# Cosformer attention into a mixture of experts on one core: routing of the last chunks behind the fourth first layer, first gates for one rank alone, a weight load moved up, last products in banks of their own

## Chip, cores and metric

One Trainium2 chip, one of its cores. The metric is the device time of one execution in microseconds (us); lower is better. The kernel before took 336.34 us (median of 3 runs, 334.81 to 336.97).

## The reference, cut to what matters

```python
# q, k, v: (8, 8, 576, 64); moe weights: w_gate, w_output_gate (512, 8), w1 (8, 512, 1024), w2 (8, 1024, 512)
attn = linear attention with cos/sin position weights      # -> x: (4608 tokens, 512)
logits = x @ w_gate
e_idx  = argmax(logits, axis=1)                            # one expert for a token
gate_w = softmax(logits)[token, e_idx]
eom    = sigmoid(x @ w_output_gate)
for e in range(8):
    m = e_idx == e
    out[m] = gate_w[m] * eom[m, e] * (relu(x[m] @ w1[e]) @ w2[e])
```

The draw is fixed. It gives the experts 305, 493, 580, 0, 986, 569, 398 and 1277 tokens.

## The kernel before

Attention runs in 36 units of 128 tokens, and its rows are written ("scattered") into regions of DRAM, one for each expert. Then the rows come back in 39 tiles of up to 128 tokens of one expert: gather (`xg`), transpose (`x_tr`), first layer, transpose (`h_tr`), second layer, output. A chunk is the 128 rows of one scatter, an eviction is VectorE's copy of a second layer's product out of PSUM (`ysb`), and a gate is a wait for a rank's weights (`wait_ge` on `wsem`). Experts are ranked; ranks 0 to 3 have their weights loaded before or about the end of attention, ranks 4 to 7 during the tiles. Tiles 0 to 7 are fixed early ("early table"); the gathers of tiles 8 and later need the late table and all scatters.

All scatters, weight loads and outputs are issued by GpSimd, on one DMA queue. The gathers are issued by SyncE. A weight load reads 2 MB of float32 and writes 1 MB of float16.

```python
def x_tr(j):                        # transpose the rows of tile j, wait for its weights
    ...
    if j < 2:
        lim = (32, 48)              # 32: rank 0 is loaded; 48: rank 1 too
    ...
    for m, n in enumerate(lim):
        DVE.wait_ge(wsem[m], n)
    DVE.tensor_copy(xts, xp16)

def layer2(j):
    ...
    yp = yps[0][:, j % 2, :]        # two banks of one PSUM tile
    ...                             # 8 matmuls, eviction on DVE (ysb)
    GP.indirect_dma_start(out=out, in_=ysb, ...)

# after attention; j counts tiles, "late" builds the late table, step() is routing of the last 5 chunks
layer1(0); x_tr(2); layer1(1); h_tr(0); ...; layer1(2); h_tr(1); x_tr(3)
step()                              # first stage, VectorE only
layer2(0); scatter(3, 2); scatter(3, 3)
step(3)                             # the stage with matmuls (rk) and what follows
layer2(1); step()
scatter(3, 4); scatter(3, 5)
for j in range(3, NMAIN + 1):
    h_tr(j - 1); x_tr(j + 1)
    for _ in range(2 if j < 6 else 0):
        next(late, None)
    layer1(j)
    for c in {3: (6, 7), 4: (8,)}.get(j, ()):
        scatter(3, c)
    layer2(j - 1)                   # (j - 2 for tiles that are transposed by DMA)
    fetch(...)                      # gathers: tiles 8 and 9 at j = 5
    for w in wload.get(j, ()):      # {4: [(4, 1)], 5: [(4, 0)], 6: [(5, 0)], ...}: (rank, half)
        load_w(*w)
```

Of the kernel before, what the change touches and what calls it, by code (L numbers as in the profile page):

```python
# [10 lines left out]
F32 = mybir.dt.float32  # L11
# [10 lines left out]
def kernel(  # L22
# [23 lines left out]
    P = 128  # L46
    NC4 = 4
    NG = B // 2
# [5 lines left out]
    NMAIN = 39  # L54
# [151 lines left out]
    def load_w(r, m):  # L206

        if r not in wreg:
            wreg[r] = GP.value_load(ordi[0:1, r:r + 1], min_val=0, max_val=E - 1)
            if r > 1:  # L210

                GP.wait_ge(wsem[r % 2], 16 * (r % 2) + 32 * (r // 2))
        er = wreg[r]
        if m == 0:
            d = GP.dma_start(w1v[:, r], moe_w1[bass.ds(er, 1)].rearrange(
                "o (c p) f -> p (o c) f", p=128))
        else:
            d = GP.dma_start(w2v[:, r], moe_w2[bass.ds(er, 1)].rearrange(
                "o (c p) d2 -> p (o c) d2", p=128))
        d.then_inc(wsem[r % 2], 16)  # L220
        tc.declare_no_dep(d.ins, group="mm", reason="ranks loaded before")
        tc.add_to_no_dep_group("w", d.ins)
# [25 lines left out]
    ptr = ctx.enter_context(tc.tile_pool(name="ptr", bufs=2, space=bass.MemoryType.PSUM))  # L248
    if True:
# [295 lines left out]
        def scatter(g, c):  # L545

            di, meta, xrows, c0, c1 = scat[g]
            if c == c0:
                GP.tensor_copy(xrows[:, c0:c1, DM:DM + 4].bitcast(F32), meta[:])
            else:  # L550
                GP.nop()
            d = GP.indirect_dma_start(
                out=xs[:, :],
                out_offset=bass.IndirectOffsetOnAxis(ap=di[:, c - c0:c - c0 + 1], axis=0),
                in_=xrows[:, c, :], in_offset=None)


            tc.declare_no_dep(d.ins, group="sc", reason="distinct rows")
            tc.declare_no_dep(d.ins, group="early", reason="distinct rows")
            tc.add_to_no_dep_group("sc", d.ins)  # L560
# [73 lines left out]
        def late_valid():  # L634

            sp = ptr.tile([P, 512], F32, name="shift", tag="tr")
            PE.matmul(sp[:, 0:NL], onesf[:], dgs[:], start=True, stop=True)
            DVE.tensor_scalar(valid[:], sp[:, 0:NL], pv[:, 0:1], None, ALU.is_le)
# [23 lines left out]
        def late_table():  # L662
            counts("l")
            yield
            ti = small("ti@l", [P, E], I32)
            DVE.tensor_scalar(ti[:], prm[:, 2, 0:E], 127.0, None, ALU.add)
            DVE.tensor_single_scalar(ti[:], ti[:], 7, op=ALU.arith_shift_right)
            tl = small("tl@l", [P, E])
            DVE.tensor_tensor(tl[:], ti[:], tk[:], ALU.subtract)
            pin = prefix("l", tl[:])  # L670
            DVE.tensor_copy(nlate[:], pin[:, E - 1:E])
            yield
            DVE.tensor_tensor(tl[:], tl[:], pin[:], ALU.subtract)
            DVE.tensor_tensor(prm[:, 0, 0:E], tl[:], tk[:], ALU.add)
            yield from table("l", tabs[1], pin)
# [3 lines left out]
        yps = []  # L679
# [13 lines left out]
        def x_tr(j):  # L693
            xg = xgs[j]
            xps = ptr.tile([P, 512], F32, name=f"xtsp{j}", tag="tr")
            xp16 = xps[:, 0:256].bitcast(F16)
            for kc in range(4):
                PE.transpose(xp16[:, kc * 128:(kc + 1) * 128],  # L698
                             xg[:, kc * 128:(kc + 1) * 128].bitcast(F16), ident16[:, :])

            if j < 2:

                lim = (32, 48)
            elif j < 22:
                tab, jj = (tabs[0], j) if j < EARLY else (tabs[1], j - EARLY)
                lim = nc.values_load_multi_w_load_instructions(
                    tab[jj:jj + 1, 0:2], engines=(mybir.EngineType.DVE,),
                    min_val=16, max_val=144)[1]
            else:
                lim = (128, 144) if j == 22 else ()  # L710
            for m, n in enumerate(lim):
                DVE.wait_ge(wsem[m], n)
            xts = fsb.tile([P, 4, P], F16, name=f"xts{j}", tag="xts")
            DVE.tensor_copy(xts[:].rearrange("p k t -> p (k t)"), xp16)  # L714
            xtss[j] = xts
            if j >= EARLY:
                jj = j - EARLY
                DVE.copy_predicated(sidx[:, jj:jj + 1], valid[:, jj:jj + 1],
                                    xg[:, DM:DM + 2].bitcast(I32))
# [36 lines left out]
        def layer2(j):  # L756
            hts = htss.pop(j)
            ev = evr.pop(j)
            xg = xgs.pop(j)
            if not yps:  # L760
                yps.append(pkv.tile([P, 2, 512], F32, name="yps", tag="kvp"))
            yp = yps[0][:, j % 2, :]
            for fc in range(8):
                mm = PE.matmul(yp, hts[:, fc, :],  # L764
                               wt[:, bass.ds(ev, 1),
                                  4 * F + fc * DM:4 * F + fc * DM + DM],
                               start=(fc == 0), stop=(fc == 7))
                tc.declare_no_dep(mm.ins, group="w", reason="waits on wsem")
                tc.add_to_no_dep_group("mm", mm.ins)
            ysb = fsb.tile([P, DM], F32, name=f"ysb{j}", tag="ysb", bufs=5)  # L770
            DVE.tensor_scalar(ysb[:], yp, xg[:, DM + 2:DM + 4].bitcast(F32),  # L771
                              None, ALU.mult)
            idx = (xg[:, DM:DM + 2].bitcast(I32) if j < EARLY
                   else sidx[:, j - EARLY:j - EARLY + 1])
            d = GP.indirect_dma_start(  # L775
                out=out[:, :],
                out_offset=bass.IndirectOffsetOnAxis(ap=idx, axis=0),
                in_=ysb[:], in_offset=None,
                bounds_check=N - 1, oob_is_err=False)
            tc.declare_no_dep(d.ins, group="so", reason="distinct rows")  # L780
            tc.add_to_no_dep_group("so", d.ins)
# [11 lines left out]
        i = 0  # L793
# [70 lines left out]
        pending = []  # L864

        def step(n=1):
            for _ in range(n):
                for p in list(pending):
                    try:
                        next(p)  # L870
                    except StopIteration:
                        pending.remove(p)

        wload = {25: [(0, 0)], 26: [(0, 1)], 28: [(1, 0)], 29: [(1, 1)], 31: [(2, 0)],
                 32: [(2, 1)], 34: [(3, 0)]}
# [4 lines left out]
        for i, (b, c) in enumerate(units):  # L880
# [58 lines left out]
            if n == 8:  # L939
                pending.append(route(g, glog, xrows, *((0, GC) if g < 3 else (4, GC))))  # L940
            else:
                step({20: 1, 21: 2, 22: 3, 23: 0, 24: 3, 25: 0, 26: 0}.get(i, 1))

            if i == 30:
                first_half = route(g, glog, xrows, 0, 4)
# [42 lines left out]
            for w in wload.get(i, ()):  # L988
                load_w(*w)

        wload = {4: [(4, 1)], 5: [(4, 0)], 6: [(5, 0)], 7: [(5, 1)], 8: [(6, 0)],
                 9: [(6, 1)], 10: [(7, 0)], 12: [(7, 1)]}
        late = late_table()

# [13 lines left out]
        x_tr(3)  # L1008
        step()
        layer2(0)  # L1010
        scatter(NG - 1, 2)
        scatter(NG - 1, 3)
        step(3)
        layer2(1)
        step()
        assert not pending
        scatter(NG - 1, 4)
        scatter(NG - 1, 5)
        for j in range(3, NMAIN + 1):
            if j < NMAIN and j - 1 not in BY_DMA:  # L1020
                h_tr(j - 1)
            if j + 1 < NMAIN:
                x_tr(j + 1)

            for _ in range(2 if j < 6 else 0):
                next(late, None)
            if j < NMAIN:
                layer1(j)
            for c in {3: (6, 7), 4: (8,)}.get(j, ()):
                scatter(NG - 1, c)  # L1030

            for m in (j - 2, j - 1):
                if (m in BY_DMA) == (m == j - 2):
                    if j == NMAIN - 1 and m == j - 1:

                        h_tr(j)
                    layer2(m)
            if j == 6:
                late_valid()
            for jj in {5: [8, 9], 6: [10, 11]}.get(j, [j + 5]):  # L1040
                if 5 <= j and jj < NSLOT:
                    fetch(jj)
            if j in BY_DMA:
                h_tr(j)
            for w in wload.get(j, ()):
                load_w(*w)
        with tc.If(nc.values_load(nlate[0:1, 0:1], min_val=0, max_val=NL) >  # L1047
                   NMAIN - EARLY):
            x_tr(NMAIN)
# [40 lines left out]
```

## Time and profile before

| | |
|---|---|
| median of 3 runs | 336.34 us |
| TensorE, VectorE, ScalarE, GpSimd busy | 90, 58, 44, 40% |
| attention's last product starts | 157.03 us |
| from there to tile 7's first layer | 42.3 us |
| from there to the end of the span | 137.9 us |

The last two rows are "the head" (from attention's last product to tile 7's first layer, 199.37 - 157.03) and "the rest" (337.3 - 199.37). The lines of the profile are in the prediction.

### The profile page before, as it was taken

To read this page: it belongs to the slowest core of one execution; us is meant where nothing else is said; L and a number is where in the kernel's file an instruction comes from. 1 tells how busy PE (TensorE), PEld (TensorE's weight loads), DVE (VectorE), ACT (ScalarE), POOL (GpSimd) and SP (SyncE) were. 2 spreads that over 40 slices of the span, in tenths; PEclk is the share of its full clock that TensorE was granted. 3 is DMA by queue.
4 is the path that set the end of the run, shared out by engine and by line. 5 is a ranking of instruction groups with operands and counts; after the bars stand their busy time and mean duration, and the time that the engine had idled before them with its cause. 6 is when DMAs were issued, how large, how long until landed. Compare 5 with 4: busy or idle time off the path is not lost. (4 is left out here: it accounts for less than half of the span.)

```text
span 337.3 us, 8923 instructions
## 1 busy us (share of the span) xinstructions
PE 303.6 (90%) x3032; PEld 198.4 (59%) x3032; DVE 194.8 (58%) x547; ACT 148.3 (44%) x253; POOL 136.5 (40%) x171
## 2 busy tenths in 40 slices
PE   7998899999999889987948789998989999999980
PEld 2577788888787778865514445554544444444530
DVE  6667568975788997965867534444343323422330
ACT  3246798877787678535301222221223232223210
POOL 7002224318833576576776443433121322232231
PEclk9999999999999999999979999999999999999997
DMA  8999999987996588999999299999997979776711
GB/s 184 312 295 313 275 230 313 235 249 205 318 247 184 167 219 156 219 221 230 228 229 232 100 196 240 225 246 254 246 245 173 200 171 191 171 172 159 174 46 47
DMA packets 83164, 71.81 MB, mean 213 GB/s; under 512 B 36078, under 2 KB 75566, under 8 KB 83120
## 3 DMA queue, kind: packets, MB, share of 16 engines
q1 hardware_dynamic: 65568, 40.17, 48.2%
q0 software_dynamic: 17552, 31.05, 41.0%
q8 instruction: 28, 0.46, 0.6%
q14 instruction: 16, 0.13, 0.1%
HBM read 67.61 MB, written 16.17 MB: 248 GB/s over the span
## 5 line engine op out<-in xcount | busy, mean ns | idle before, releaser
L754 ACT ACTIVATE hs<-hp 128x1024 f16<-128x1024 f32 x39 | 39.9, 1023 | 116.9 <-PE hp L746 107.7
L764 PE MATMUL yps<-wt,hts 128*128 x312 | 75.0, 384 | 3.7 <-DVE ysb L771 1.5
L771 DVE TENSOR_SCALAR ysb<-yps,xg 128x512 f32<-128x512 f32 x39 | 29.3, 751 | 83.1 <-PE yps L764 78.0
L746 PE MATMUL hp<-wt,xts 128*128 x312 | 73.7, 379 | 3.3 <-DVE xts L714 2.0
L468 POOL TENSOR_TENSOR xr<-wt,rc 128x512 f16<-128x512 f32 x36 | 40.5, 1132 | 66.7 <-DVE rc L464 59.4
L775 POOL DMA_INDIRECT out_dram<-ysb,sidx x31 | 30.2, 975 | 79.4 <-DVE ysb L771 76.8
L764 PEld LDWEIGHTS <-hts 128*128 128x128 f16 x312 | 30.8, 99 | 41.6 <-issue 4.8
L445 PE MATMUL qo<-kvm,wt 64*128 64x162 f32 (+1 forms) x640 | 50.5, 310 | 3.2 <-DVE wt L453 2.2
L746 PEld LDWEIGHTS <-xts 128*128 128x128 f16 x312 | 29.1, 98 | 31.6 <-DVE xts L714 2.2
L445 PEld LDWEIGHTS qo<-kvm,wt 64*128 64x128 f32 (+1 forms) x640 | 40.7, 175 | 10.2 <-DVE wt L453 3.7
L451 ACT ACTIVATE wt<-qo,cosc 128x324 f32<-128x324 f32 x72 | 36.9, 528 | 19.7 <-PE qo L445 17.1
L453 DVE SCALAR_TENSOR_TENSOR wt<-qo,sinc,wt 128x324 f32<-128x324 f32 x72 | 37.0, 550 | 12.9 <-ACT wt L451 8.5
L427 PE MATMUL qtp<-ident,wt 128*64 128x128 f32 x576 | 40.0, 279 | 0.5 <-ACT wt L406 0.5
L427 PEld LDWEIGHTS qtp<-ident,wt 128*64 128x64 f32 x576 | 30.9, 136 | 7.5 <-issue 6.5
L382 PE MATMUL kvp<-wt 128*64 128x130 f32 x448 | 31.2, 277 | 0.9 <-ACT ktr L335 0.8
L382 PEld LDWEIGHTS kvp<-wt 128*64 128x64 f32 x448 | 25.3, 136 | 2.3 <-issue 1.1
L714 DVE COPY xts<-xtsp 128x512 f16<-128x512 f16 x39 | 16.3, 420 | 13.4 <-DMA wt<-in_moe_w_dram 5.2
L431 DVE TENSOR_SCALAR wt<-qtp 128x512 f32<-128x512 f32 x32 | 21.8, 681 | 1.4 <-PE qtp L427 1.4
L336 ACT ACTIVATE wt<-wt,cosc 128x512 f32<-128x512 f32 x28 | 20.0, 713 | 0.6 <-DMA wt<-in_v_dram 0.6
L335 ACT ACTIVATE wt<-wt 128x512 f32<-128x512 f32 x28 | 17.5, 624 | 1.9 <-PE kvp L382 1.9
L340 ACT ACTIVATE wt<-wt,sinc 128x512 f32<-128x512 f32 x24 | 17.2, 715 | 0.0
L698 PE MATMUL xtsp<-ident,xg 128*128 128x128 f16 x156 | 14.9, 219 | 1.4 <-DMA xg<-xs 1.4
(271 smaller groups left out, 302.1 us busy)
## 6 DMA issues: line engine op xcount, KB each, us to landing
wt<-in_moe_w_dram POOLq DMA_DIRECT2D x16, 1024.0 KB
wt<-in_k_dram SPq DMA_DIRECT2D x16, 512.0 KB
wt<-in_v_dram SPq DMA_DIRECT2D x16, 512.0 KB
wt<-in_q_dram SPq DMA_DIRECT2D x16, 512.0 KB
xg<-xs SPq DMA_DIRECT2D x43, 129.0 KB
xs<-zt SPq DMA_DIRECT2D x9, 129.0 KB
wt<-in_k_dram SPq DMA_DIRECT2D x8, 128.0 KB
vtb<-in_v_dram SPq DMA_DIRECT2D x8, 128.0 KB
```

The lines of the kernel that those rows point to most:

```text
L382: PE.matmul(kvp[64 * ab:64 * ab + 64, s_ // 2, o:o + 130], kr[p0:p1, head(s_, ab), :], vw[p0:p1, head(s_, ab), :], start=(c == 0 and s_ % ...
L427: PE.matmul(tp[64 * ab:64 * ab + 64, 128 * s_:128 * s_ + 128], src[:, head(s_, ab), :], ident[:], start=True, stop=True)
L431: DVE.tensor_scalar_max(qT2[i % 2], tps, 0.0)
L445: PE.matmul(qo[t0:t1, 2 * ab + s_, 0:162], qT[r0:r0 + 64, s2, t0:t1], kvms[b if c < 4 else b - 1 + j][r0:r0 + 64, 2 * s2:2 * s2 + 2, :], s ...
L451: d0 = ACT.activation(t, qo[:, :, 0:81], AF.Copy, scale=cosc[:, c:c + 1])
L453: d1 = DVE.scalar_tensor_tensor(u[:, h0:h0 + 4, :], qo[:, :, 81:162], sinc[:, c:c + 1], t, ALU.mult, ALU.add)
L468: GP.tensor_tensor(xrows[:, slot + x, 0:DM].bitcast(F16).rearrange("p (h d) -> p h d", d=D), u[:, 8 * x:8 * x + 8, 0:64], rc[:, 8 * x:8 * ...
L746: mm = PE.matmul(hp[:, fh * 512:fh * 512 + 512], xts[:, kc, :], wt[:, bass.ds(ev, 1), kc * F + fh * 512:kc * F + fh * 512 + 512], start=(k ...
L754: ACT.activation(hs[:], hp, AF.Relu)
L764: mm = PE.matmul(yp, hts[:, fc, :], wt[:, bass.ds(ev, 1), 4 * F + fc * DM:4 * F + fc * DM + DM], start=(fc == 0), stop=(fc == 7))
L771: DVE.tensor_scalar(ysb[:], yp, xg[:, DM + 2:DM + 4].bitcast(F32), None, ALU.mult)
L775: d = GP.indirect_dma_start(out=out[:, :], out_offset=bass.IndirectOffsetOnAxis(ap=idx, axis=0), in_=ysb[:], in_offset=None, bounds_check= ...
```

## The change

The intent: take the routing's matmuls out of TensorE's way (they stood ahead of tile 1's second layer), start tiles 0 and 1 when rank 0's weights are there, fill a hole in the DMA with an earlier weight load, and free the last two second layers of a wait for the eviction before them. The early routing steps are also dealt out anew.

```diff
@@ x_tr
-                lim = (32, 48)
+                lim = (32,)
@@ layer2
-            yp = yps[0][:, j % 2, :]
+            if NMAIN - 2 <= j < NMAIN:
+                yp = ptr.tile([P, 512], F32, name=f"yp{j}", tag="tr")[:]
+            else:
+                yp = yps[0][:, j % 2, :]
@@ attention units
-                step({20: 1, 21: 2, 22: 3, 23: 0, 24: 3, 25: 0, 26: 0}.get(i, 1))
+                step({20: 2, 21: 0, 22: 2, 23: 0, 24: 3, 25: 1, 26: 0}.get(i, 1))
@@ loads
-        wload = {4: [(4, 1)], 5: [(4, 0)], 6: [(5, 0)], ...
+        wload = {3: [(4, 1)], 5: [(4, 0)], 6: [(5, 0)], ...
@@ tiles
         scatter(NG - 1, 3)
-        step(3)
         layer2(1)
-        step()
-        scatter(NG - 1, 4)
-        scatter(NG - 1, 5)
         for j in range(3, NMAIN + 1):
             ...
-            for _ in range(2 if j < 6 else 0):
-                next(late, None)
             if j < NMAIN:
                 layer1(j)
-            for c in {3: (6, 7), 4: (8,)}.get(j, ()):
+            if j == 3:
+                step(4)
+            for _ in range({3: 1, 4: 2, 5: 3}.get(j, 0)):
+                next(late, None)
+            for c in {3: (4,), 4: (5, 6), 5: (7, 8)}.get(j, ()):
                 scatter(NG - 1, c)
+            for w in wload.get(j, ()):
+                load_w(*w)
             ...                      # layer2, fetch
-            for w in wload.get(j, ()):
-                load_w(*w)
```

In GpSimd's order this puts the load (4,1), half of rank 4, ahead of the scatters of chunks 5 to 8. The kernel before issues it behind all of them.

More of the change, by code (lines that the diff above doesn't have):

```diff
@@ L989 @@
                 load_w(*w)
-        wload = {4: [(4, 1)], 5: [(4, 0)], 6: [(5, 0)], 7: [(5, 1)], 8: [(6, 0)],
+        wload = {3: [(4, 1)], 5: [(4, 0)], 6: [(5, 0)], 7: [(5, 1)], 8: [(6, 0)],
                  9: [(6, 1)], 10: [(7, 0)], 12: [(7, 1)]}
@@ L1012 @@
         scatter(NG - 1, 3)
-        step(3)
         layer2(1)
-        step()
-        assert not pending
-        scatter(NG - 1, 4)
-        scatter(NG - 1, 5)
         for j in range(3, NMAIN + 1):
@@ L1023 @@
                 x_tr(j + 1)
-            for _ in range(2 if j < 6 else 0):
-                next(late, None)
             if j < NMAIN:
                 layer1(j)
-            for c in {3: (6, 7), 4: (8,)}.get(j, ()):
+            if j == 3:
+                step(4)
+                assert not pending
+            for _ in range({3: 1, 4: 2, 5: 3}.get(j, 0)):
+                next(late, None)
+            for c in {3: (4,), 4: (5, 6), 5: (7, 8)}.get(j, ()):
                 scatter(NG - 1, c)
+            for w in wload.get(j, ()):
+                load_w(*w)
             for m in (j - 2, j - 1):
```

## The prediction

> **What bounds the kernel now.** I read the page first, then TensorE's idle time in order of time, then VectorE and GpSimd where TensorE waits, then busy time in stretches of 1 us for the DMA share.
>
> ```profile
> PE   7998899999999889987948789998989999999980
> DMA  8999999987996588999999299999997979776711
> ```
>
> Each digit is 8.4 us. TensorE is at 8 or 9 nearly everywhere; its weak slices are number 20 and 21 (160 to 177 us) and a few after them. The DMA engines are full from about 120 to 250 us, but for one slice, the "2" at 185 to 194 us. Attention ends at 158 us; then 39 tiles of 128 tokens follow, each a first layer (line 746) and a second (line 764). The tiles run at a beat of 4.12 us up to number 17 (193.65 for tile 6 against 189.53 for tile 5) and 3.68 us later (304.86 to 308.53). From 231 us to the last tiles TensorE has one idle of 0.90 us and no other, so what is gained before it can reach the end, if no wait swallows it on the way.
>
> The timeline of TensorE (start, duration, then in brackets the idle time before it):
>
> ```profile
> 157.03 1.34 PE L445 MATMUL qo<-kvm,wt 64*64 64x162 f32 x32 [0.24 <-DVE wt L453]
> 160.35 1.89 PE L746 MATMUL hp<-wt,xts 128*128 x8 [1.99 <-DVE xts L714]
> ...
> 173.24 0.20 PE L511 MATMUL rk<-oh,u 128*128 128x48 f16 x1 [4.49 <-DVE oh L503]
> 173.81 3.15 PE L764 MATMUL yps<-wt,hts 128*128 x8 [0.25 <-DVE ysb L771]
> 177.47 1.89 PE L746 MATMUL hp<-wt,xts 128*128 x8
> ...
> 198.57 0.40 PE L698 MATMUL xtsp<-ident,xg 128*128 128x128 f16 x4 [0.71 <-DMA xg<-xs]
> 199.37 1.89 PE L746 MATMUL hp<-wt,xts 128*128 x8 [0.40 <-issue]
> ...
> 229.41 0.40 PE L698 MATMUL xtsp<-ident,xg 128*128 128x128 f16 x4 [0.67 <-DMA xg<-xs]
> 230.21 1.89 PE L746 MATMUL hp<-wt,xts 128*128 x8 [0.40 <-issue]
> ```
>
> The reader is to see three kinds of loss: waits on VectorE at 158 and 169 us (1.99, 4.49 and 0.25), a second layer at 3.15 instead of 1.89 us, and two waits for gathered rows (xg, tiles 8 and 15). The same view at the end of the span shows the last two second layers waiting for evictions:
>
> ```profile
> 324.48 1.89 PE L764 MATMUL yps<-wt,hts 128*128 x8 [0.40 <-DVE ysb L771]
> 327.21 1.89 PE L764 MATMUL yps<-wt,hts 128*128 x8 [0.84 <-DVE ysb L771]
> ```
>
> VectorE's timeline for the first two waits:
>
> ```profile
> 159.77 0.76 DVE L714 COPY xts<-xtsp 128x512 f16<-128x512 f16 x2 [2.32 <-DMA wt<-in_moe_w_dram]
> 170.67 1.73 DVE L497 TENSOR_TENSOR oh@3_4_2622<-glog,lmax@3_4_2618 128x40 f32<-128x40 f32 x1
> 172.90 0.20 DVE L503 TENSOR_TENSOR oh<-iota8m,ei@3_4_2625 128x40 f16<-128x40 f32 x1
> 173.02 0.74 DVE L771 TENSOR_SCALAR ysb<-yps,xg 128x512 f32<-128x512 f32 x1
> ```
>
> The copy at 159.77 waited for the weights of rank 1, though tiles 0 and 1 use rank 0. That rank 0 is there sooner: the load of rank 2 is issued at 151.28 behind a wait for rank 0. And the eviction at 173.02 stands behind the routing's first stage in VectorE's order.
>
> GpSimd's timeline, where all scatters (552), weight loads (215, 218) and outputs (775) are issued:
>
> ```profile
> 142.98 1.04 POOL L552 DMA_INDIRECT xs<-xr,di@2_0_2158  x1 [0.28 <-POOL xr L549]
> 160.42 1.00 POOL L552 DMA_INDIRECT xs<-xr,di@2_0_2158  x1 [2.76 <-DMA xs<-xr,di@2_0_2158]
> 186.73 0.98 POOL L552 DMA_INDIRECT xs<-xr,di@3_4_2679  x1 [0.30 <-issue]
> 192.02 0.94 POOL L218 DMA_DIRECT2D wt<-in_moe_w_dram  x1 [0.94 <-PE hp L746]
> ```
>
> The issue at 160.42 waits for the DMA eight before it, by the instruction order the scatter of 142.98. That scatter, 128 rows, took 17 us: it was done just after rank 1's weights, issued right ahead of it, had landed at 159.7. So a scatter behind a weight load waits for the load. And in busy time by 1 us, the hole in the DMA:
>
> ```profile
> 189.00:190.00 1.00, 1.00 (x13) 0.68 (x11) 0.93 (x2) 0.00 (x0) 0.00 (x0) 1.00 0.00 0
> ```
>
> The last two columns are the DMA share and GB/s: nothing moves between the last scatter (186.73) and the next weight load (192.02).
>
> **What the Trainium skill says.** "TensorE: Matmul & The Clock Gate", Part 1: after an idle window of about 3.4 us the array runs at half clock until it has been busy for such a window. The trace agrees: granted clock 0.50 from 173 to 176 us, after the 4.49 us of idle. "SBUF — State Buffer", section "SBUF: two separate sides": VectorE and GpSimd share a port pair as an exclusive lock; the other fully blocks. The trace agrees: line 497 took 1.73 us instead of the 0.20 of its neighbours, and ended at 172.40 with GpSimd's line 468 (171.28 to 172.33). "DMA: Bandwidth & Descriptors", section "Queues, rings and completion order": on each DMA engine, descriptors are consumed in ring order. The scatter of 142.98 agrees; this one carries my prediction.
>
> **The change, part by part.**
>
> *First gates for rank 0 alone.* The copies at 159.77 can follow the last line 453 before them (ends 157.46): xts0 is ready at about 157.9, before attention's last product ends at 158.37. The first layer starts there: -1.99 us.
>
> *Routing behind the fourth first layer.* Only its later stages move. The first stage (lines 491 to 503) keeps its place ahead of the eviction of tile 0 on VectorE, and the second layer of tile 1 waits for that eviction, since both outputs are halves of one buffer (the 0.25 of before). So most of the 4.49 stays: everything shifts by 1.99, and if GpSimd's line 468 no longer meets line 497, 1.5 more is gone. TensorE then idles from 166.8 to about 170.5, 3.7 us, so the half clock may or may not come. I take the second layer of tile 1 at 170.5 to 171.5 and the first layer of tile 3 at about 173.3: -4.2 us. From there to tile 7's first layer before took 21.9 us, of which 16.5 are four beats, the rest late evictions and tile 8's rows. With late routing spread over tiles 3 to 5, I count about 18 us (VectorE still delays one second layer by some 0.7): tile 8's rows would be wanted at about 191 and tile 7 could start near 192, -7.4 us in all.
>
> *Weight loads.* Half of rank 4 (4,1) is issued after tile 3's first layer, about 179 instead of 192 us, into the hole. But it now stands ahead of four scatters (chunks 5 to 8), and tile 8's gather waits for the last of these. The second half of rank 3 lands at about 181 (GB/s jumps to 330 and 400 at 181 to 183, which are plain copies). Then in ring order: three scatters and two outputs, 0.9 MB, at about 350 GB/s 2.6 us; the 1 MB load, about 5 us (four loads took 24 us with other traffic from 160); 1.05 MB of outputs and scatters, 3 us. That is 191.6, and a microsecond for completion: the gather is issued at about 192.5, where it was issued at 192.95 before. It landed 5.6 us later then. So tile 8's rows come at about 198, and of the 7.4 us some 6.5 turn into a longer wait there. Tile 7 starts at 198.7 or so: -0.7 us.
>
> *After it.* Tile 15's rows wait for the output of tile 7 (its buffer), which before was behind (4,1), (4,0), (5,0), (5,1), counted from 194 when the DMA restarts, to 223.6: 29.6 us. After the change it is behind (4,0), (5,0), (5,1), (6,0), since loads are now issued ahead of outputs: as much data, but from 192. So 221.6, rows at 227; tile 14 reaches them at 227.3 and starts at about 228, against 230.21: -2.2 us. Beyond that TensorE is the bound as before.
>
> *Last products in banks of their own.* The waits of 0.40 and 0.84 go: -1.24 us, straight off the end.
>
> *Early routing steps* (units 20 to 26) move four VectorE operations away from a stall of 1.17 us at 112 us to a place just ahead of a copy on the chain. I give it 0, within 0.7, and what comes of it is swallowed at tile 8.
>
> Sum: 2.2 + 1.24 = 3.4 us; 336.34 - 3.4 = 332.9, rounded to 333.0.
>
> **Rivals.** *The queue does not hold the scatters up* (they overlap with the load). Then tile 8's rows come at about 191 to 193 and the 7.4 us reach the end, with 1.24 more: 327.7 us. For it: the table of late tiles is ready at about 187 instead of 191.84. Against: the scatter of 142.98. *The queue costs more*: (4,1) and the gathers share full DMA engines and each output is one load further back; if tile 8's rows come at 200.5 and tile 15's at 230.5, nothing but the tail is left or less: 335 to 336.5. For it: DMA share 1.1 from 195 to 248 us. *The old VectorE stage keeps everything*: the idle crosses the clock window again, so tile 3 gains 2 instead of 4 us; as the rows of tile 8 set the pace, that makes 333 all the same.
>
> **Range and chances.** The two DMA steps decide. Both at their worst give 336, the rival without queueing 327.7; I take 329.0 to 336.0. Faster by over 2% needs 329.6 or less: that takes at least half of the swallowed time to come through, 0.15. Slower by 2% needs 343, which nothing here makes: 0.02. Within: 0.83.
>
> **What would show it.** Right: first layer of tile 0 at 158.4 us; the idle before tile 1's second layer still 3 to 4.5 us and released by the eviction; no DMA hole at 185 to 194; a wait of 4 to 7 us for xg before tile 8's transposes, or a gather issued at about 192; no idle between the last three second layers. Wrong: tile 8's rows at 193 or sooner (then about 328), or a first layer of tile 14 later than 230 (then 335 or more).

## The result, and the profile after

The changed kernel took 344.49 us (median of 4 runs, 344.13 to 345.46); the kernel before 335.67 us in the same session. Ratios here are the mean time of one kernel's fast runs over that of the other's of the same rounds, so not quite the ratio of these medians: 1.0264, with a 95% interval of 1.0219 to 1.0309. The change makes the kernel slower by 2.6%.

The profiled spans are 337.3 us before and 342.6 us after, 5.3 us apart and not 8.8: the profiled run of before (338.99 us) was slower than all its timed ones. The head grew from 42.3 to 52.5 us; the rest shrank from 137.9 to 134.5 us.

TensorE's timeline after the change, the lines that answer to those shown before:

```profile
157.33 1.89 PE L746 MATMUL hp<-wt,xts 128*128 x8 [0.45 <-issue]
...
171.47 3.57 PE L768 MATMUL yps<-wt,hts 128*128 x8 [5.69 <-DVE ysb L775]
...
176.12 1.92 PE L746 MATMUL hp<-wt,xts 128*128 x8
...
206.90 0.61 PE L698 MATMUL xtsp<-ident,xg 128*128 128x128 f16 x4 [13.45 <-DMA xg<-xs]
208.02 2.99 PE L746 MATMUL hp<-wt,xts 128*128 x8 [0.51 <-issue]
...
330.52 3.62 PE L768 MATMUL yp<-wt,hts 128*128 x16
```

Tile 0 starts at once (0.45 instead of 1.99 us). Tile 1's second layer waits even longer than before, and for the eviction. Tile 8's rows then keep TensorE idle for 13.45 us, and the first layer after that runs partly at half clock (2.99 us). From there to the end there is no idle at all: the waits of before at tiles 13 to 15, at 245 us and at the last two second layers (now 16 matmuls in one piece) are gone. That is 4.5 us; less 1.1 us for the slow first layer, it is the 3.4 us of the rest.

VectorE after the change: the first stage of the routing, the eviction, and the end of the late table:

```profile
168.33 1.73 DVE L497 TENSOR_TENSOR oh@3_4_2620<-glog,lmax@3_4_2616 128x40 f32<-128x40 f32 x1
...
170.68 0.75 DVE L775 TENSOR_SCALAR ysb<-yps,xg 128x512 f32<-128x512 f32 x1
...
188.21 0.15 DVE L631 TENSOR_TENSOR tab<-cj@l,sel@l 128x1 int32<-128x1 f32 x1
```

The table is ready at 188.4, as against 191.84 before. GpSimd after the change: scatter of chunk 4, the load (4,1), and the last scatter:

```profile
181.98 0.98 POOL L552 DMA_INDIRECT xs<-xr,di@3_4_2736  x1 [0.86 <-POOL xr L549]
183.86 0.94 POOL L218 DMA_DIRECT2D wt<-in_moe_w_dram  x1 [0.90 <-DMA xs<-xr,di@3_0_2537]
...
191.54 0.97 POOL L552 DMA_INDIRECT xs<-xr,di@3_4_2736  x1 [0.30 <-issue]
```

And SyncE: the gather of tile 8 before the change, the gathers from that of tile 8 on after it, and from the list of SyncE's waits after it (us in total, times, longest) the one for the last scatters:

```profile
192.95 0.34 SPq L688 DMA_DIRECT2D xg<-xs  x1
```

```profile
200.40 5.40 SPq L688 DMA_DIRECT2D xg<-xs  x5
```

```profile
SPq L688 <- DMA xs<-xr,di@3_4_2736: 11.2, 1, 11.2
```

So the gather of tile 8 goes out at 200.40, 12 us after the table is ready, and for 11.2 of them it waits for the scatters, the last of which was issued at 191.54. In the kernel before, SyncE's list has no wait for these scatters; the gather follows the table (191.84) by 1.1 us. The trace's packet records say when they moved: the load (4,1) from 185.5 to 193.9 us, the scatters of chunks 5 to 8 with two outputs between them from 193.3 to 198.6. In the kernel before, the last scatter moved at 188.3 to 189.1, and the load from 193.7 to 202.6. The page's list of DMA issues gives the median time from issue to landing of the 16 weight loads in its last column, which the page of the kernel before does not have:

```profile
wt<-in_moe_w_dram POOLq DMA_DIRECT2D x16, 1024.0 KB, 12.6
```

### The profile page after: what moved, and what is told of

Read it like the earlier page. It is cut to its first block, busy times and chain, and to the rows that moved or that the text cites. A ratio compares the mean times of both kernels' runs of the same rounds, so it can differ in the third digit from the quotient of the medians.

```text
span 342.6 us, 8922 instructions
## 1 busy us (share of the span) xinstructions
PE 302.7 (88%) x3032; PEld 198.9 (58%) x3032; DVE 194.2 (57%) x547; ACT 148.5 (43%) x253; POOL 136.9 (40%) x171
## 5 line engine op out<-in xcount | busy, mean ns | idle before, releaser
L768 PE MATMUL yps<-wt,hts 128*128 x296 | 71.6, 386 | 6.1 <-DVE ysb L775 5.7
L746 PE MATMUL hp<-wt,xts 128*128 x312 | 74.8, 383 | 1.0 <-issue 1.0
L775 DVE TENSOR_SCALAR ysb<-yps,xg 128x512 f32<-128x512 f32 x37 | 27.8, 750 | 75.2 <-PE yps L768 75.2
L779 POOL DMA_INDIRECT out_dram<-ysb,sidx x31 | 30.2, 973 | 83.8 <-DVE ysb L775 83.0
L714 DVE COPY xts<-xtsp 128x512 f16<-128x512 f16 x39 | 16.3, 420 | 25.0 <-PE xtsp L698 14.2
L698 PEld LDWEIGHTS <-xg 128*128 128x128 f16 x156 | 11.4, 100 | 18.5 <-DMA xg<-xs 13.6
## 6 DMA issues: line engine op xcount, KB each, us to landing
wt<-in_moe_w_dram POOLq DMA_DIRECT2D x16, 1024.0 KB, 12.6
```

The lines of the kernel that those rows point to most:

```text
L698: PE.transpose(xp16[:, kc * 128:(kc + 1) * 128], xg[:, kc * 128:(kc + 1) * 128].bitcast(F16), ident16[:, :])
L746: mm = PE.matmul(hp[:, fh * 512:fh * 512 + 512], xts[:, kc, :], wt[:, bass.ds(ev, 1), kc * F + fh * 512:kc * F + fh * 512 + 512], start=(k ...
L768: mm = PE.matmul(yp, hts[:, fc, :], wt[:, bass.ds(ev, 1), 4 * F + fc * DM:4 * F + fc * DM + DM], start=(fc == 0), stop=(fc == 7))
L775: DVE.tensor_scalar(ysb[:], yp, xg[:, DM + 2:DM + 4].bitcast(F32), None, ALU.mult)
L779: d = GP.indirect_dma_start(out=out[:, :], out_offset=bass.IndirectOffsetOnAxis(ap=idx, axis=0), in_=ysb[:], in_offset=None, bounds_check= ...
```

## The experiments

My theory after the result: a scatter completes only after a load issued before it on the same queue, so the load put ahead of the scatters holds up the gather of tile 8. Rivals: the early load takes DMA bandwidth from what it meets, whatever the order; or the routing and its table come too late. Times are medians, with that of the kernel before on the same chip. "Gather" is SyncE's issue of tile 8's gather, and "from attention" the same counted from attention's last product, which is what can be compared across runs; "wait" is TensorE's idle before tile 8's transposes.

| run | us | before | ratio (95%) | gather, us | from attention | wait, us | head | rest |
|---|---|---|---|---|---|---|---|---|
| before | | 336.34 | 1 | 192.95 | 35.9 | 0.71 | 42.3 | 137.9 |
| changed | 344.49 | 335.67 | 1.0264 (1.0219 to 1.0309) | 200.40 | 44.9 | 13.45 | 52.5 | 134.5 |
| a1_loads_back | 346.79 | 338.86 | 1.0220 (1.0172 to 1.0269) | 202.02 | 45.1 | 9.94 | 52.0 | 135.2 |
| a2_load_behind | 342.51 | 338.86 | 1.0092 (1.0044 to 1.0140) | 194.20 | 36.0 | 0.46 | 43.4 | 137.3 |
| a3_scatters_first | 340.54 | 338.86 | 1.0034 (0.9985 to 1.0083) | 194.66 | 37.2 | 0.78 | 44.9 | 135.8 |
| b1_load_early | 345.42 | 338.86 | 1.0156 (1.0103 to 1.0209) | 197.93 | 41.1 | 8.10 | 49.5 | 137.6 |
| d1_double_load | 349.01 | 335.85 | 1.0384 (1.0346 to 1.0422) | 204.21 | 48.7 | 18.03 | 55.9 | 136.0 |
| p1_gates | 335.38 | 335.85 | 0.9984 (0.9948 to 1.0020) | 190.95 | 33.8 | 2.68 | 41.5 | 136.4 |
| p2_banks | 335.10 | 335.85 | 0.9977 (0.9949 to 1.0005) | 189.74 | 34.1 | 2.56 | 41.9 | 134.8 |
| e1_stage_behind | 336.68 | 335.85 | 1.0044 (1.0002 to 1.0085) | 185.27 | 30.2 | 0.54 | 35.4 | 143.5 |
| e2_loads_after_outputs | 338.82 | 338.70 | 0.9994 (0.9949 to 1.0039) | 194.40 | 37.2 | 1.58 | 45.3 | 133.3 |
| e3_loads_spread | 342.55 | 338.70 | 1.0030 (0.9945 to 1.0114) | 192.00 | 33.9 | 3.60 | 41.7 | 140.3 |
| f1_gates_banks | 338.57 | 338.53 | 0.9967 (0.9912 to 1.0023) | 193.90 | 36.5 | 2.79 | 44.8 | 135.0 |
| f2_changed_again | 346.18 | 338.53 | 1.0226 (1.0165 to 1.0288) | 200.14 | 43.4 | 9.60 | 50.6 | 134.8 |

All gave correct results. Three of e3's timed runs were slow; its median is of all, its ratio of the fast ones. The changed kernel, a1, b1, d1 and f2 are slower clear of noise, the changed kernel and d1 by more than 2% for certain; a2 is slower by 0.9%, e1 by 0.4% and hardly clear of noise.

The gather, the wait, the head and the rest come from one profiled run each. They move without an edit: the head is 41.5 us in p1 and 44.8 in f1, which share its code, and 45.3 in e2 and 41.7 in e3, whose code differs only from tile 6 on. So differences of under some 4 us in the head are not read.

**a1_loads_back**: the changed kernel, with the loads where the kernel before has them, behind the outputs. (4,1) is then issued later, at tile 4, but still ahead of the scatters of chunks 7 and 8.

```diff
-        wload = {3: [(4, 1)], 5: ...
+        wload = {4: [(4, 1)], 5: ...
-            for w in wload.get(j, ()):     # ahead of layer2
-                load_w(*w)
+            for w in wload.get(j, ()):     # at the end of the iteration
+                load_w(*w)
```

> The changed kernel with the weight loads put back where the kernel before has them: (4,1) at the end of tile 3+1's iteration, all loads after the outputs. Scatters of chunks 7 and 8 are still issued after (4,1). Theory (in GpSimd's queue a scatter completes only after a load issued before it): the scatter of chunk 8 still lands some 13 us after the load's issue, so the gather of tile 8 is issued at 200 us or later and the wait for xg stays above 10 us; 342 to 348 us. Rival (the harm is the load coming early and taking DMA bandwidth, or the routing coming late): most of the loss goes, 332 to 337 us.

Measured: the load came 3.9 us later than in the changed kernel (issue at 187.71; 2.5 us later counted from attention's last product) and the kernel was as slow. The scatter of chunk 8 moved only from 196.6 to 198.5, behind the load's 189.4 to 197.8. The wait was 9.94 us and not above 10, since TensorE had lost 2.95 us at two places before it. Moving the load by this little doesn't help as long as it stays ahead of a scatter. Late routing, the other half of the rival, is untouched here; a2, a3 and b1 test it.

**a2_load_behind**: the changed kernel, with (4,1) behind the scatters of chunks 7 and 8.

```diff
-        wload = {3: [(4, 1)], 5: [(4, 0)], ...
+        wload = {5: [(4, 1), (4, 0)], ...
```

> The changed kernel with (4,1) issued in tile 5's iteration, behind the scatters of chunks 7 and 8, just ahead of (4,0). Theory: the gather of tile 8 goes out when the last scatter has landed and the table is ready, at 190 to 193 us; the wait for xg is 0 to 5 us instead of 13.5; 329 to 334 us. Rival (late routing is what delays the gather): the gather still goes out near 200 us and the time stays above 340 us.

```profile
194.20 4.25 SPq L688 DMA_DIRECT2D xg<-xs  x4
```

Measured: the gather went out at 194.20, counted from attention 8.9 us sooner than in the changed kernel, and the wait fell from 13.45 to 0.46 us. The wait overstates it: TensorE had lost 4.26 us to a late relu just before and so came to tile 8 later. The time did not reach 329 to 334: 342.51 us, 1.0092 of the kernel before on this slower chip. In the profiled run the gather now waits for the table (the last scatter was through at 192.5), and the table was held up by a stall of 3.61 us on VectorE at 188 us, while ScalarE started that relu some 5 us after its input; the profile calls the releaser of both "remote". The rest is 2.8 us longer than in the changed kernel, as the rows of two later tiles are waited for again (1.00 and 1.31 us). Whether these make up the whole 0.9% is not shown.

**a3_scatters_first**: the changed kernel, with all late scatters ahead of (4,1), in the same iteration, so that the load stays early.

```diff
-            for c in {3: (4,), 4: (5, 6), 5: (7, 8)}.get(j, ()):
+            for c in {3: (4, 5, 6, 7, 8)}.get(j, ()):
```

> The changed kernel with all five late scatters issued in tile 3's iteration, directly ahead of (4,1), which so stays early. Theory: order alone matters; the last scatter lands by about 190 us, the gather goes out then, its rows share the DMA engines with (4,1) and come at 193 to 197 us; the wait for xg is 1 to 5 us; 329 to 334 us. Rival (the early load takes the bandwidth): the wait stays near 10 us; 338 us or more.

GpSimd's, VectorE's and TensorE's lines of this run: the last scatter directly ahead of the load; the end of the table; the wait for tile 8:

```profile
188.32 0.97 POOL L552 DMA_INDIRECT xs<-xr,di@3_4_2736  x1 [0.30 <-issue]
189.28 0.96 POOL L218 DMA_DIRECT2D wt<-in_moe_w_dram  x1
```

```profile
193.67 0.15 DVE L631 TENSOR_TENSOR tab<-cj@l,sel@l 128x1 int32<-128x1 f32 x1
```

```profile
201.57 0.40 PE L698 MATMUL xtsp<-ident,xg 128*128 128x128 f16 x4 [0.78 <-DMA xg<-xs]
```

The scatters were through at 190.4 and the load moved from 191.0 to 198.6. The gather went out 37.2 us after attention's last product, not 44.9 as in the changed kernel (35.9 before). Its rows moved from 198.3 on, when the load was about through, and tile 8's transposes began 6.9 us after the gather's issue; it was 6.5 in the changed kernel and 5.6 before. So the load may cost the gather itself about 1 us, while the order costs the 8 us before it. The wait of 0.78 us again overstates the gain, as TensorE had just lost 3.53 us to a late relu. The ratio fell to 1.0034 from 1.0264 and 1.0226, measured on other chips: about 2%. It falls short of the expected 329 to 334 us for the reason of a2: the table was ready only at 193.8, because VectorE stood still for 2.90 us before the copy ahead of its last part.

**b1_load_early**: the kernel before with (4,1) moved up by one tile, which puts it ahead of the scatter of chunk 8. One part of the change alone.

```diff
-        wload = {4: [(4, 1)], 5: ...
+        wload = {3: [(4, 1)], 5: ...
```

> The kernel before with (4,1) alone moved one tile up, so that it is issued ahead of the scatter of chunk 8; nothing else changed. Theory: the scatter of chunk 8 lands 12 to 14 us after the load's issue, the gather of tile 8 goes out near 200 us instead of 193, and the time grows by 5 to 9 us, to 341 to 345 us. Rival (the loss of the changed kernel comes from its late routing): within 2 us of the kernel before.

GpSimd (the load, then the last scatter) and TensorE:

```profile
186.12 0.94 POOL L218 DMA_DIRECT2D wt<-in_moe_w_dram  x1 [0.32 <-issue]
187.37 1.01 POOL L552 DMA_INDIRECT xs<-xr,di@3_4_2679  x1 [0.30 <-issue]
```

```profile
205.50 0.61 PE L698 MATMUL xtsp<-ident,xg 128*128 128x128 f16 x4 [8.10 <-DMA xg<-xs]
```

The scatter moved at 194.5 to 196.3, behind the load's 187.8 to 196.0, and the gather went out at 197.93 (near 200 was expected), 5.2 us later from attention than in the kernel before. The kernel before, with its own routing, becomes 1.6% slower by this one line. So the loss does not need the late routing.

**d1_double_load**: the changed kernel with both halves of rank 4 ahead of the scatters.

```diff
-        wload = {3: [(4, 1)], 5: [(4, 0)], ...
+        wload = {3: [(4, 1), (4, 0)], ...
```

> The changed kernel with both halves of rank 4 issued ahead of the scatters of chunks 5 to 8, instead of one: the suspected cost doubled. By the packet records one such load takes 7.5 to 9 us from first to last packet, and loads in a row start 6 us apart. Theory (queue order): the gather of tile 8 goes out 6 to 8 us later than in the changed kernel (200.4), so at 206 to 209 us, the wait for xg grows from 13.5 to about 20 us, and since the loads that follow are then earlier, the time grows by 4 to 8 us over the changed kernel. Rival (some other cause of the wait): the wait stays at 13 to 14 us.

```profile
210.61 0.61 PE L698 MATMUL xtsp<-ident,xg 128*128 128x128 f16 x4 [18.03 <-DMA xg<-xs]
```

The two loads moved from 184.6 to 197.3 and the last scatter at 201.6; the gather went out at 204.21, 3.8 us later than in the changed kernel, and the time was 349.01. The wait and the time grew as the theory wants, the gather by less than the 6 to 8 us expected: in this run attention had ended at about the same place and everything before was 1 us earlier, and the second load ended only 5.5 us after the first.

**p1_gates** and **p2_banks**: the two small parts alone, on the kernel before.

```diff
-                lim = (32, 48)
+                lim = (32,)
```

> The kernel before with the first gates for rank 0 alone, nothing else. Prediction's step: the first layer of tile 0 starts within 0.5 us of attention's end instead of 2 us after it, and tiles 1 to 3 follow 1 to 2 us earlier; but the gather of tile 8 still waits for the table and the scatters, so at most 1.5 us reach the end: ratio 0.994 to 1.000. Rival (the gates stand on the path to the end): 2 us, 0.994 or less.

```diff
-            yp = yps[0][:, j % 2, :]
+            if NMAIN - 2 <= j < NMAIN:
+                yp = ptr.tile([P, 512], F32, name=f"yp{j}", tag="tr")[:]
+            else:
+                yp = yps[0][:, j % 2, :]
```

> The kernel before with the last two second layers in banks of their own, nothing else. Prediction's step: the waits of 0.40 and 0.84 us at the end go, 1.2 us, ratio 0.996, and no other idle appears there.

Tile 0 in p1_gates, the same in p2_banks, which has the old gates, and tile 8 in p1_gates:

```profile
158.98 1.89 PE L746 MATMUL hp<-wt,xts 128*128 x8 [0.48 <-issue]
```

```profile
157.45 1.89 PE L746 MATMUL hp<-wt,xts 128*128 x8 [0.45 <-issue]
```

```profile
197.90 0.40 PE L698 MATMUL xtsp<-ident,xg 128*128 128x128 f16 x4 [2.68 <-DMA xg<-xs]
198.70 3.50 PE L746 MATMUL hp<-wt,xts 128*128 x8 [0.40 <-issue]
```

With the new gates tile 0 starts within 0.48 us of attention's end. But p2 has the old ones and starts it within 0.45: there rank 1's weights, whose last packet moved at 155.0 us and not at 157.5 as in the kernel before, were in time. In b1, also with the old gates, the wait is 1.09 us. So the 1.99 us are what one run lost, and what the gates are worth is not shown. The wait for tile 8 is 2.68 us in p1 and 2.56 in p2, where it was 0.71 in the kernel before, and the first layer behind it is slow in both (3.50 and 3.25 us); so that can't be put down to the gates either. With p2 the waits of 0.40 and 0.84 us at the end are gone and no other appears. Both ratios have an interval that includes 1; their size is as expected, but neither is shown to be faster by the times alone.

**e1_stage_behind**: a3 with the routing's first stage moved, on VectorE, behind the evictions of tiles 0 and 1.

```diff
-        x_tr(3); step(); layer2(0)
+        x_tr(3); layer2(0)
             if j + 1 < NMAIN:
                 x_tr(j + 1)
+            if j == 3:
+                step()
             if j < NMAIN:
                 layer1(j)
```

> The changed kernel with all late scatters ahead of (4,1), as in the run that did so, and with the routing's first stage on VectorE moved behind the evictions of tiles 0 and 1, the transposed copies of tile 2 and the gates of tile 4. If that stage is what tile 1's second layer waits for: its wait falls from 5 us to at most 1 us and the second layer takes 1.9 us instead of 3.5, so the first layer of tile 3 starts near 171 us instead of 176 to 177; a wait of 1 to 3 us for the routing's first stage appears behind it. The gather goes out 2 to 5 us earlier. 330 to 336 us here where the kernel before takes about 337 to 339. Rival (what is gained there is swallowed at tile 8): within 1 us of the run with scatters first.

```profile
167.59 1.89 PE L768 MATMUL yps<-wt,hts 128*128 x8 [2.30 <-DVE ysb L775]
173.46 0.18 PE L511 MATMUL rk<-oh,u 128*128 128x48 f16 x1 [1.58 <-DVE oh L503]
...
204.01 0.40 PE L698 MATMUL xtsp<-ident,xg 128*128 128x128 f16 x4 [4.60 <-DMA xg<-xs]
```

The wait of tile 1's second layer fell from 5 to 2.30 us (1 was expected), it ran at full clock, and tile 3's first layer began at 169.99. The gather went out at 185.27, so the head is 35.4 us, 6.9 shorter than before. But the rest is 143.5, 5.6 longer: tile 10's rows waited 4.60 us. Their buffer comes free with the output of tile 2, and that output now stands behind (4,1) in GpSimd's queue (issue at 185.80, load at 184.56). So the same mechanism took back what the head had gained. 336.68 us: 330 to 336 was expected beside a kernel before of 337 to 339, which took 335.85 here, so the expectation was missed.

**e2_loads_after_outputs**: e1 with the loads at the end of each iteration, behind the outputs. **e3_loads_spread**: also with the loads of ranks 5 to 7 spread over more tiles.

```diff
-        wload = {3: [(4, 1)], 5: [(4, 0)], 6: [(5, 0)], 7: [(5, 1)], 8: [(6, 0)],
-                 9: [(6, 1)], 10: [(7, 0)], 12: [(7, 1)]}
+        wload = {3: [(4, 1)], 5: [(4, 0)], 7: [(5, 0)], 9: [(5, 1)], 10: [(6, 0)],
+                 12: [(6, 1)], 13: [(7, 0)], 15: [(7, 1)]}      # e3 only
```

> The previous kernel (late scatters first, routing's first stage behind the evictions) with every weight load issued behind the output of its iteration instead of ahead of it; (4,1) stays in tile 3's iteration. Theory (a gather waits for the output that frees its buffer, and that output waits in GpSimd's queue for any load ahead of it): the wait of 4.6 us for tile 10's rows goes, tile 10's first layer starts 5 us earlier; the rows of tiles 13 to 15 then wait 1 to 6 us in all, since four loads still stand ahead of the output of tile 7; 329 to 333 us where the kernel before takes 336. Rival (DMA bandwidth alone sets when these rows come): the waits only move to later tiles, 335 to 337 us.

> The same with the loads of ranks 5 to 7 put 1 to 3 tiles later (tiles 7, 9, 10, 12, 13, 15), so that only three loads stand ahead of the output of tile 7. Theory: the waits of tiles 13 to 15 shrink by one load, some 6 us, to about nothing; all weights are wanted only at tile 22, about 250 us, and land at 245 to 252; 326 to 331 us. Rival: the last load is late at tile 22 and gives it back there, 331 us or more.

In e2 the wait for tile 10's rows is gone, as expected, and nothing waits after tile 8: its rest, 133.3 us, is the shortest of all. But its head was 45.3 us and not 35: tile 1's second layer waited 3.37 us and ran at half clock again, and TensorE waited 1.57 us for VectorE and 2.82 us for ScalarE at tiles 4 to 6. Ratio 0.9994. In e3 the last load moved until 254.1. TensorE lost 0.59 us at tile 20, whose copy on VectorE waited by the profile for weights, and 2.64 us at 257 us for the transpose of tile 18, which goes by DMA. At tile 22, which wants all weights, nothing waited. So something is given back, as its rival said, but at other tiles; that the late load delayed the transpose is not shown. Both miss their expected time. They were run on another chip than e1, whose head I could not repeat, so which lengthened the head, chip, edit or the chance between runs, is open.

**f1_gates_banks**: the kernel before with p1 and p2 together, which leave GpSimd's queue alone. **f2_changed_again**: the changed kernel once more, unedited, on a further chip.

> The kernel before with the two parts of the change that do not touch the order of GpSimd's queue: first gates for rank 0 alone, last products in banks of their own. Theory: the gates' gain is mostly swallowed at tile 8 (ratio alone 0.998), the banks' 1.2 us reach the end (alone 0.998): together 0.993 to 0.998, the fastest of the versions here. Rival: both were noise, 0.999 to 1.001.

> The changed kernel itself once more, on another chip. If its loss is one of the program and not of a chip: ratio 1.02 to 1.03, the gather of tile 8 at 199 to 203 us, the wait for xg above 11 us.

f1 comes out at 0.9967 (0.9912 to 1.0023), the lowest ratio of the versions here, but not shown to be faster. f2 repeats the loss, 1.0226, with the gather at 200.14; the wait is 9.60 us instead of 13.45 (above 11 was expected), as TensorE had lost 3.33 us at tile 5 already.

## Why the prediction was wrong

It said 333.0 us and at most 336.0, and gave 0.02 to a kernel slower by over 2%; the change costs 8.8 us. Of its steps:

- **First gates**: not settled. Tile 0 starts at once, but in p2 it does so with the old gates too; 1.99 us was one run's wait, taken for a fixed cost.
- **Routing**: right that the first stage keeps its place and that tile 1's second layer waits for the eviction behind it (5.69 us, released by the eviction). Wrong that tile 3 would gain 4.2 us. I had hoped that GpSimd's line 468 would miss VectorE's line 497; it shifted with it and met it again (1.73 us). In both kernels line 497 began 0.6 us before line 468 and ended with it; that GpSimd's instruction held the one that had begun sooner is inferred from the common end alone. And the longer idle brought half clock for the whole of that second layer (3.57 us). From attention's last product to tile 3's first layer it took 20.6 us after and 20.4 before: the gain was 0.
- **Weight loads, the step that failed**: "the 1 MB load, about 5 us (four loads took 24 us with other traffic from 160)", and with it "That is 191.6, and a microsecond for completion: the gather is issued at about 192.5". The order was right: the scatters waited for the load. The terms were mis-sized, the load's own and its start. Those four loads moved from 156.9 to 182.6 by the packet records, starting some 6 us apart but each taking 8.2 to 8.5 us from first to last packet: they overlap. A scatter behind a load is through only after the load's last packet, so the rate of a row of loads was the wrong number to use for one of them. The sum as it came out: the load began to move at 185.5 where I had 183.6 (issued 4.9 us later than I thought, since the chunk's routing came later), took 8.4 us where I had 5, the scatters and outputs behind it 4.7 us where I had 3, and completion and issue 1.8 us where I had 0.9. That makes 200.4 instead of 192.5. As attention's last product started 1.5 us earlier in this run than in the kernel before, the start was in truth 3.4 us late and not 1.9, as much as the load was too long. The rows then took 6.5 us to come, 5.6 before.
- **The wait that follows**: with tile 8 wanted at 193.5 (I had 191) the wait is 13.45 us where I named 4 to 7 as what would show the step right. The half clock behind it costs about another 1.1 us (2.83 instead of 1.72 us to the next product).
- **Tile 15's rows**: could not be judged; with tile 7 some 9 us later than I had it, no later tile waits for its rows. The rest became 3.4 us shorter: the last two products account for 1.24 and the waits of tiles 13 to 15 and at 245 us for about 3, less the 1.1 us of the slow first layer.
- **Banks**: right, 0.40 and 0.84 us, straight off the end.
- **Early routing steps**: 0 within what can be seen; attention's last product starts between 155.67 and 157.45 us with the old ones and between 155.07 and 158.25 with the new. They were not run alone.

Two readings of the record were off as well, without weight: of the slices "20 and 21 (160 to 177 us)" only the second is weak (a 4; the first is a 9), and in the hole something did move: the last scatter itself until 189.1 and an output from 191.7; it was empty for 2.5 us between them.

Of my rivals, "the queue costs more" had the direction but not the reason: it let the load and the gathers share the DMA engines, up to 336.5 us, and took the same 5 us for granted. Run b1 shows that the order with its earlier load makes most of the loss in the kernel before, a1 that a later load doesn't help while a scatter stays behind it, a2 and a3 that changing the order takes the long wait for the scatters away, with the load late or early, and d1 that a second load adds to it. The order accounts for 1.3 to 2.3 points of the 2.3 to 2.6%; the 0.9% left in a2 has no shown cause.

What stays open: the stalls of 2 to 5 us on ScalarE and VectorE near 188 to 193 us, for which the profile names "remote" or an instruction that had ended; the kernel before has such stalls as well, and they may decide whether a2, a3 and e2 beat it. No version here is shown to be faster than the kernel before.

## What to carry to other kernels

On one DMA queue, by what GpSimd's did here, a small transfer that something waits for must be issued ahead of a large one that nothing waits for, even where that leaves a hole: here one line (b1), meant for a stretch of 8 us in which the DMA engines were two tenths busy, cost 5.3 us by its ratio (3.5 to 7.1). When a wait will end with a transfer in a queue, size it by the time from that transfer's first packet to its last, not by the rate at which several of them go through. And where an earlier finish frees a buffer for the next gather, follow the chain once more: e1 lost behind an output what it had gained before a scatter.

## What the Trainium skill lacked or had wrong

- "DMA: Bandwidth & Descriptors", section "Queues, rings and completion order": its ring order is borne out, also for GpSimd's queue (the paragraph is on those of SyncE and ScalarE), but it gives no time for a small transfer behind a large one. Here the scatters began 0.6 to 2.1 us before the load's last packet (193.3 against 193.9 after the change, 194.5 against 196.0 in b1, 195.7 against 197.8 in a1), so that nearly the load's whole duration is added.
- The same page, section "Bandwidth", gives 6.15 us for a 1 MB transfer from HBM to SBUF without more. A load that writes 1 MB and casts it from 2 MB took 6.1 to 10.9 us from first to last packet in these runs, mostly 7 to 9, beside the kernel's other traffic, and from issue to landing a median of 12.6 to 14.2 us in the five runs whose page has it. The page has no figure for a load that casts.
- No page that I read explains the stalls of ScalarE and VectorE above (3.61 us on VectorE in a2, releaser "remote").
